# Attention, token mixing and gated convolution on one core: values' buffers written once, decoding apart from the sums, and a new order

## The chip, the core and the metric

One NeuronCore of a Trainium2 chip runs the whole program. Its engines work side by side, each on a queue of its own in program order: TensorE (PE, with PEld for its weight loads), VectorE (DVE), ScalarE (ACT), GpSimd (POOL) and SyncE (SP), which issues DMAs. The metric is the device time of one execution in microseconds; lower is better. The kernel before takes 675.87 us, the median of three runs (673.92 to 677.92).

## The reference

Four batches of eight heads with 576 tokens and 64 columns per head go through attention with a causal mask and a bias from cumulated sums; the heads' outputs are put side by side (512 columns), mixed over tokens, then over channels, then gated by a convolution over five tokens:

```python
scores = scale * q @ k.T + min(-(cum[:, None] - cum[None, :]), 0)   # causal
attn = softmax(scores);  x = concat_heads(attn @ v)
u = x + (relu(x.T @ w_tok1) @ w_tok2).T         # 576 -> 256 -> 576, over tokens
x = u + relu(u @ w_ch1) @ w_ch2                 # 512 -> 1536 -> 512
out = (sigmoid(conv5(x, conv_w)) * (x @ w_val)) @ w_out
```

The weights arrive as float64, two 32-bit words per number, and are decoded on the chip; q, k, v and s are float32. Products of float32 are made of three products of float16: each operand is split into a high part and a rest, scaled so that nothing underflows.

## The kernel before

**Tiles.** A batch b is worked as four pairs of heads (named b_0 to b_3), each over five tiles of at most 128 tokens; keys grow with the tile (causal). Batch 0's pairs are "wide": their product with v is a float32 one. A pair loads q, k and v, finds their largest values, scales and splits them (`qk16`, `v16`), transposes q and k by DMA (`turn_qk`, which gives `qkT` and `qk2`), writes a row of scales into `qk2` (`fill`), makes scores S on PE, masks and takes the maximum on DVE, exponentiates on ACT, splits p, transposes it (`p_turn`, tile pT; by DMA or on PE), and multiplies with v into the one PSUM bank `xbank` (`av`). `norm` reads the row sums out of xbank and inverts them on DVE; `x_value` multiplies. Then come token mixing (`tok1`, `tok2`), and for each batch two chunks of tokens (320 and 256, named b_0 and b_1) with the channel product: `u_split` (u from R, on DVE), `ch1` (matmuls `c<-u`), `ch2` (`c<-hT`), convolution and gate, `val` and `outp`.

**Weights.** A weight arrives in pieces `raw` of 128 rows with two words per number. `decode` (line 698) is given one piece: ACT scales the high word into `top` (a PSUM bank, or the weight's place in `arena` if the piece is longer than 512), ACT prepares the low word in place, DVE joins both into `arena`, PE sums the piece's columns with a matrix of ones (`ws_*<-arena,ones`, function `summed`, for the scale of the weight), and then the sign is put in: by DVE, or by ACT and a product on GpSimd. `scale` reads the sums' bank; `split` makes the high part and the rest.

**Values' buffers.** `load_v` of a wide pair takes a buffer of tag `v16`, has GpSimd write zeros into the rows behind the last token and ones into the 65th column (so that the product with v gives the row sums too), and then issues three DMAs on SP. A pair that is not wide loads v into `vst` and makes `v16` in `split_v`.

**What sets the order.** Every piece of work is a task, a generator that yields the engine of its next step. The text `ORDER` lists all steps by hand or search, an engine's letter and a task's number: V138 is the next step of task 138 on DVE. `Plan.run` replays it, so it is the program order of all five queues. Ahead of a step on PE, `keep_warm` compares the planned busy share of PE with `WARM_FILL` and puts filler matmuls in (`plan.idle`, line 524: `xbank<-ones`, 128x112, into columns 400 to 512 of xbank, which nobody reads). The dependency is kept for a tile, so a reader of xbank in program order behind a filler waits for the filler too. Where a task may choose its engine (`fillers`, `signed`, `one`, `two`), the letter in `ORDER` decides. The functions `cost_*` are the plan's own prices; they set how many fillers it inserts.

Everything that the engines are told goes through one call, so most rows of the profile carry line 256 (255 in the changed kernel); fillers carry 524 (525).

Of the kernel before, what the change touches and what calls it, by code (L numbers as in the profile page):

```python
# [8 lines left out]
F32 = mybir.dt.float32  # L9
# [9 lines left out]
SIGN = -(2 ** 31)  # L19
# [18 lines left out]
    fill=dict(V=(0.26, 130), A=(0.83, 200)),  # L38
# [14 lines left out]
WARM_FROM, WARM_FILL, GAP1 = 12e3, 0.65, 13.87  # L53
# [27 lines left out]
S6 S9 G138 S138 P7 A10 A10 V10 P10 A10 G10 S0 V0 P1 V1 V1 P1 V1 V1 S11 S17 A12 A12 A8 A8 V8 A2 A3 P8 V2 A3 A8 A2 V12  # L81
S137 A140 A140 A140 P12 V2 S20 V12 V3 P141 V141 V141 P141 V141 V141 V141 A142 V142 A143 V143 G8 V13 V13 V14 V14 S26
P18 A19 A19 V19 A21 A21 V21 P19 V19 P21 V21 V22 V22 P27 V25 S2 S139 S31 A28 A28 V28 G190 P28 S29 A30 A30 V30 A32 V28
A145 P30 V30 S191 A32 S144 S190 S144 P146 V146 P168 V168 P148 V148 A147 P154 V154 A169 P152 V152 A153 A155 P170 G4
S33 P160 V160 S189 S45 G24 G24 A149 V32 A34 S40 P174 V174 P177 P156 A156 P32 V32 A34 P156 A156 V177 A192 P150 A161
A150 A192 A192 G15 V34 V170 A171 P178 P175 V175 A176 P158 G5 G5 G5 G5 P34 V34 V35 V35 S43 P41 A46 P156 A156 P193
V193 P172 A172 V193 P151 P151 A42 P193 P172 A172 P157 V158 A159 V178 A179 V193 V193 V193 P157 G16 G16 P172 P162 A162
A46 V195 V194 V195 V194 P180 A180 S241 P162 A162 A42 V42 P162 A162 V197 P180 V46 A172 G15 P163 P163 V164 V164 V165
G23 A39 P42 P46 V46 A180 P180 A44 A44 V44 P173 P173 S47 A48 A48 P44 V42 S196 A180 P181 P181 G23 V44 V48 V166 V166
V182 V182 A183 G36 G37 P48 S196 P198 V198 A199 P212 V212 P200 V200 P206 V206 A184 A201 G37 S61 A48 S68 P167 A167  # L90
P204 V204 A205 V184 G36 G242 S242 P220 P226 V226 A213 P202 A207 P210 V210 P229 V229 G48 V49 A202 G39 V220 S54 P186
P186 A211 A186 V186 P230 P185 A185 P214 A214 S57 P227 V230 S59 V227 V49 A244 A244 A244 P187 P187 V187 V188 V188 P214
P55 A58 P245 V245 V245 P222 V222 S293 A214 P208 P245 V245 A208 V245 V245 V246 V188 V246 P69 P208 G247 V247 P214 A58
V58 S243 S248 S248 V249 A208 P208 A221 A208 A223 A228 P203 P203 P209 P209 P224 A214 P215 P215 V216 V216 V217 V218
V218 G50 A56 A231 G50 P232 G52 P58 V58 A224 P224 A56 V56 A232 A224 P232 A232 P224 A224 P232 A70 A70 V70 P219 P225
P225 P56 V56 P70 A232 P233 P233 G294 S294 S295 V70 S71 A60 A62 A62 V62 A60 V60 P62 A219 A38 G38 V234 V234 A235 P250
V250 A251 A51 P256 V256 A257 P258 V258 A259 P278 P281 V281 P264 V264 A265 P252 V252 A253 P60 V60 S73 S467 V62 S75
V278 P260 A260 P254 A236 V236 P260 A260 P272 V272 G53 P279 V279 P262 V262 A254 A296 G53 P274 V274 A296 P282 A273
P238 P238 V63 A296 P297 V297 V297 P297 V282 V297 S466 V297 V297 G299 A275 A72 A72 V72 P260 A260 V298 P255 P255 V299
P276 A263 P266 V298 P72 P261 P261 A280 V63 V65 S300 V67 A266 P266 V72 S77 G65 A74 A238 V238 S300 A74 V74 A266 P266  # L100
A283 P284 A266 P267 P267 V268 V268 A284 A76 A276 P276 A76 V76 A276 P284 A284 P237 V269 V270 V270 A237 A469 G66 P276
# [354 lines left out]
def gated_block_kernel(  # L456
# [241 lines left out]
    def decode(a, raw, tag, summed=None):  # L698
# [16 lines left out]
        if summed is not None:  # L715
            yield from summed()
        yield signed(n)
        x = ti if inner else raw[:, :, 1]
        if plan.engine is A:
            A.activation(low.bitcast(F32), x.bitcast(F32), AF.Sign)  # L720
            if inner:
# [1027 lines left out]
```

## Time and profile before

| | |
|---|---|
| median of three runs | 675.87 us (673.92 to 677.92) |
| profiled execution, time | 676.46 us |
| its span in the trace | 674.6 us (1.86 us outside) |
| PE busy | 616.4 us, 91%, 6040 matmuls |
| DVE busy | 509.1 us, 75%, 1400 |
| ACT busy | 383.9 us, 57%, 796 |
| GpSimd busy | 229.6 us, 34%, 336 |
| chain that ended last | PE 58%, DVE 15%, DMA 8%, ACT 4%, issue 3% |

Busy time is the union of an engine's instructions. PEclk is the share of TensorE's full clock (2.4 GHz) that was granted; 0.50 is 1.2 GHz. In a timeline row the number in brackets is the engine's idle time just before it, and what ended that. A buffer number is left out of a name, so `arena<-top,raw` stands for many pieces. The first channel product (`c<-u`) begins at 151.17 us; what lies before it is called the front.

### The profile page before, as it was taken

The numbers are of one execution on the slowest core, as the hardware profiler recorded it, in microseconds if no ns is written. First come the engines' busy times: TensorE is split into PE (matmuls) and PEld (weight loads), VectorE is DVE, ScalarE is ACT, GpSimd is POOL, SyncE is SP. The second block draws the span as 40 slices with busy tenths as digits, with TensorE's granted clock in tenths as the row PEclk, the third lists the DMA queues.
The fourth block names the chain that finished last, engine by engine and source line by source line (L and its number), as shares of the span: only waits on it lengthen the run. The fifth ranks groups of instructions, "written<-read, shape, count | busy, mean of one in ns | idle before, by whom it ended". The sixth has DMA issues, their size and how long they took to land.

```text
span 674.6 us, 15836 instructions
## 1 busy us (share of the span) xinstructions
PE 616.4 (91%) x6040; PEld 491.3 (73%) x6040; DVE 509.1 (75%) x1400; ACT 383.9 (57%) x796; POOL 229.6 (34%) x336
## 2 busy tenths in 40 slices
PE   2889889876999888999989999989999999999997
PEld 2678778764777777767767777767877887678864
DVE  5785799896898988758888978777779861456472
ACT  5694889785676747566575564546575611213324
POOL 2362248331554222441426224233373200037100
PEclk9996899998999999999999999999999999999999
DMA  7977278675856646773467365844654400000002
GB/s 211 218 203 221 60 185 228 177 160 116 218 88 102 132 97 119 126 144 90 97 111 141 64 116 117 153 86 100 125 106 85 94 21 1 17 1 1 2 32 95
DMA packets 190807, 75.18 MB, mean 111 GB/s; under 512 B 178213, under 2 KB 181381, under 8 KB 190730
## 3 DMA queue, kind: packets, MB, share of 16 engines
q1 hardware_dynamic: 190730, 74.16, 50.4%
q8 instruction: 47, 0.77, 0.5%
q14 instruction: 30, 0.25, 0.1%
HBM read 33.89 MB, written 4.83 MB: 57 GB/s over the span
## 4 chain that ended last, share of the span: by engine, by line
PE 58%; DVE 15%; DMA 8%; ACT 4%; issue 3%; SPq 2%; POOL 1%; DVEq 0%; POOLq 0%; ACTq 0%
PE c L256 32%; PE o L256 6%; PE xbank L256 5%; PE v L256 4%; PE t L256 4%; DMA pT<-p 4%; PE S L256 4%; DVE x L256 3%; DVE gate L256 3%; DMA qkT<-qk 2%; SPq L256 2%; DMA qk<-qkT 2%; DVE arena L256 2%; DVE qk L256 1%; ACT x L256 1%
## 5 line engine op out<-in xcount | busy, mean ns | idle before, releaser
L256 PEld LDWEIGHTS <-arena 128*128 128x128 f16 x3168 | 287.6, 98 | 74.8 <-issue 5.3
L256 PE MATMUL c<-hT,arena 128*128 128x256 f16 (+1 forms) x1152 | 159.2, 286 | 1.3 <-DVE st L256 1.3
L256 PE MATMUL c<-u,arena 128*128 128x256 f16 (+1 forms) x1152 | 158.4, 288 | 0.7 <-DVE u L256 0.5
L256 ACT ACTIVATE x<-x,st 128x320 f32<-128x320 f32 (+4 forms) x160 | 85.7, 556 | 74.8 <-DVE st L256 72.6
L256 POOL TENSOR_TENSOR p<-x,p 128x320 f16<-128x320 f32 (+4 forms) x78 | 60.7, 780 | 113.7 <-ACT p L256 80.5
L256 DVE CUSTOM_DVE_ANT_0 x<-S,mask,sc 128x448 f32<-128x448 f32 (+4 forms) x160 | 74.7, 485 | 26.2 <-PE S L256 15.6
L256 ACT ACTIVATE hT<-c 128x320 f16<-128x320 f32 (+1 forms) x96 | 36.7, 402 | 65.4 <-PE c L256 65.2
L256 PE MATMUL xbank<-v,pT 128*128 128x65 f16 (+1 forms) x880 | 64.9, 213 | 7.2 <-DMA pT<-p 7.0
L256 DVE SCALAR_TENSOR_TENSOR hT<-c,hT 128x320 f16<-128x320 f32 (+1 forms) x96 | 41.9, 449 | 33.7 <-ACT hT L256 33.7
L256 DVE SCALAR_TENSOR_TENSOR gate<-R,cwt,gate 128x320 f32<-128x320 f32 (+1 forms) x104 | 61.0, 601 | 1.5
L256 PE MATMUL S<-qk 67*128 67x288 f16 (+4 forms) x192 | 50.9, 286 | 5.3 <-DMA qk<-qkT 5.2
L256 PE MATMUL v<-x,arena 128*128 128x256 f16 (+1 forms) x384 | 53.6, 286 | 1.8 <-DVE st L256 1.8
L256 PE MATMUL S<-qkT 128*128 128x288 f16 (+4 forms) x192 | 50.8, 284 | 2.5 <-DVE hT L256 1.6
L256 PEld LDWEIGHTS <-pT 128*128 128x128 f16 x960 | 37.7, 98 | 12.8 <-DMA pT<-p 8.9
L256 PE MATMUL o<-arena,g 128*128 128x512 f16 x192 | 45.0, 379 | 0.0
L524 PE MATMUL xbank<-ones 128*128 128x112 bf16 x433 | 36.6, 231 | 4.5 <-DVE x L256 2.6
L256 POOL TENSOR_SCALAR p<-x 128x192 f16<-128x192 f32 (+4 forms) x40 | 17.2, 429 | 63.0 <-ACT x L256 36.4
L524 PEld LDWEIGHTS <-ones 128*128 128x128 bf16 x433 | 31.0, 110 | 6.8 <-issue 4.6
L256 ACT ACTIVATE p<-x 128x448 f16<-128x448 f32 (+4 forms) x65 | 31.7, 496 | 6.1 <-DMA pT<-p 4.5
L256 PEld LDWEIGHTS <-g 128*128 128x128 f16 x192 | 18.7, 99 | 18.2
L256 ACT ACTIVATE gate<-gate 128x1280 f32<-128x1280 f32 (+1 forms) x24 | 27.8, 1160 | 7.2 <-DVE gate L256 6.8
L256 PE MATMUL t<-xn,arena 128*128 128x128 f16 x480 | 30.4, 220 | 1.1 <-DVE hT L256 1.0
(204 smaller groups left out, 1091.2 us busy)
## 6 DMA issues: line engine op xcount, KB each, us to landing
raw<-in_moe_w_ch_dram SPq DMA_DIRECT2D x24, 512.0 KB
stg<-in_q_dram SPq DMA_DIRECT2D x16, 288.0 KB
stg<-in_k_dram SPq DMA_DIRECT2D x16, 288.0 KB
qk<-qkT SPq DMA_DIRECT2D x32, 144.0 KB
out_dram<-ot SPq DMA_DIRECT2D x16, 256.0 KB
vst<-in_v_dram SPq DMA_DIRECT2D x24, 128.0 KB
raw<-in_moe_w_val_dram SPq DMA_DIRECT2D x4, 512.0 KB
raw<-in_moe_w_out_dram SPq DMA_DIRECT2D x4, 512.0 KB
```

The lines of the kernel that those rows point to most:

```text
L256: return f(*a, **k)
L524: plan.idle = lambda: nc.tensor.matmul(xbank[:, 400:512], lhsT=ones, rhs=ones[:, 0:112], start=True, stop=True)
```

## The change

1. The two buffers of tag `v16` are allocated once (`v16s`), with a list of the free ones (`free_v`). A new task `t_v` writes the zeros and ones into both on GpSimd. `load_v` of a wide pair is left with its DMAs on SP; `largest` also waits for `t_v`.
2. `decode` writes the joined word into the raw piece in place, and only the step with the sign writes `arena`: on DVE from top and raw, or as a product on GpSimd of two words of raw, the second written by ACT. The sums on PE read the raw piece (its upper 16 bits, every fourth 16-bit word, before every second one of `arena`) and stand behind the sign's step in program order. The raw piece is given back after both.
3. `fill` may run on GpSimd; in the new order two fills go from ACT and three from DVE to GpSimd, three from ACT to DVE.
4. In the plan's prices a DMA transpose is longer (150 + 180 per block, before 100 per block), other DMAs move at 320 bytes per ns (360), a transposition on PE counts 0.4 as activity (0.6), and `WARM_FILL` is 0.75 (0.65).
5. `ORDER` is a new one, with 3457 steps (3461). The number of fillers goes from 433 to 514; ahead of the first channel product from 408 to 498. All other matmuls are the same in number and size.

```diff
-    fill=dict(V=(0.26, 130), A=(0.83, 200)),
+    fill=dict(V=(0.26, 130), A=(0.83, 200), G=(0.72, 285)),
...
-WARM_FROM, WARM_FILL, GAP1 = 12e3, 0.65, 13.87
+WARM_FROM, WARM_FILL, GAP1 = 12e3, 0.75, 13.87
...
-S6 S9 G138 S138 P7 A10 A10 V10 P10 A10 G10 S0 V0 P1 V1 V1 P1 V1 V1 S11 S17 A12 A12 A8 A8 V8 A2 A3 P8 V2 A3 A8 A2 V12
...
@@ decode
         yield V
-        V.scalar_tensor_tensor(ai, ti, 3, low, ALU.logical_shift_left, ALU.bitwise_or)
-        if summed is not None:
-            yield from summed()
+        V.scalar_tensor_tensor(low, ti, 3, low, ALU.logical_shift_left, ALU.bitwise_or)
         yield signed(n)
-        x = ti if inner else raw[:, :, 1]
         if plan.engine is A:
-            A.activation(low.bitcast(F32), x.bitcast(F32), AF.Sign)
+            high = raw[:, :, 1].bitcast(F32)
+            A.activation(high, ti.bitcast(F32), AF.Sign)
             if inner:
                 give("B")
             yield G
-            G.tensor_tensor(a, a, low.bitcast(F32), ALU.mult)
+            G.tensor_tensor(a, low.bitcast(F32), high, ALU.mult)
         else:
-            V.scalar_tensor_tensor(ai, x, SIGN, ai, ALU.bitwise_and, ALU.bitwise_or)
+            V.scalar_tensor_tensor(ai, ti, SIGN, low, ALU.bitwise_and, ALU.bitwise_or)
             if inner:
                 give("B")
+        if summed is not None:
+            yield from summed()
         give(tag)
...
-                x = a.bitcast(BF16).rearrange("p (n t) -> p n t", t=2)[:, :, 1]
+                x = raw.bitcast(BF16).rearrange("p n (w t) -> p n w t", t=2)[:, :, 0, 1]
...
+    v16s = [ap.tile([P, 4 * NK * DV], F16, tag=f"v16_{i}", name=f"v16_{i}") for i in range(BUFS["v16"])]
+    free_v = list(v16s)
+
+    def wide_v(t):
+        return t.bitcast(F32).rearrange("p (h n d) -> p h n d", h=2, n=NK)
...
+    def init_v():
+
+        for t in v16s:
+            yield G
+            G.memset(wide_v(t)[TAIL:, :, NK - 1, 0:D], 0.0)
+            G.memset(wide_v(t)[:, :, :, D:DV], 1.0)
...
-            yield G, "v16"
-            t = ap.tile([P, 4 * NK * DV], F16, tag="v16", name=f"v_{self.nm}", bufs=BUFS["v16"])
-            self.vst = t.bitcast(F32).rearrange("p (h n d) -> p h n d", h=2, n=NK)
-
-            G.memset(self.vst[TAIL:, :, NK - 1, 0:D], 0.0)
-            G.memset(self.vst[:, :, :, D:DV], 1.0)
-            yield SY
+            yield SY, "v16"
+            self.vt = free_v.pop(0)
+            self.vst = wide_v(self.vt)
```

How the order moves, at the places that the prediction speaks of. Names ending in a number are allocations; `sums_0` belongs to a pair's `norm`, `su` and `u_b_c` to a chunk's `u_split`, `S` and `x_4` to scores, `arena<-top,raw` and `raw<-top,raw` to decoding, `arena<-arena,wsgs` to splitting a weight.

DVE at the begin of batch 0's channel product, before:

```order
L256 SCALAR_TENSOR_TENSOR arena<-top,raw 128x512
L256 ISA x_4_2235,st_4_2089<-S_4_1_2325,mask,st_4_2089,sc_0_1706 128x288
L256 ISA st_4_2089 128x1
L256 SCALAR_TENSOR_TENSOR u_0_0_2358<-R_121,su_2283,u_0_0_2358 128x640 x2
L256 TENSOR_SCALAR sums_0_2444<-xbank,sc_0_1706 128x6
L256 SCALAR_TENSOR_TENSOR qk_1_1_2310<-stg_1_1650,sg_1_2223,qk_1_1_2310 128x9x64
```

DVE at the same place, after:

```order
L255 SCALAR_TENSOR_TENSOR raw<-top,raw 128x512
L255 TENSOR_SCALAR sums_0_2414<-xbank,sc_0_1666 128x6
L255 RECIPROCAL sg_1_2283<-gm_1_2282 128x3
L255 SCALAR_TENSOR_TENSOR arena<-top,raw 128x512
L255 SCALAR_TENSOR_TENSOR sc_1_2284<-sg_1_2283,gck 128x1
L255 SCALAR_TENSOR_TENSOR sc_1_2284<-gm_1_2282 128x1
L255 TENSOR_SCALAR sc_1_2284<-two_107,sg_1_2283 128x2
L255 SCALAR_TENSOR_TENSOR u_0_0_2422<-R_121,su_2323,u_0_0_2422 128x640 x2
L255 ISA x_4_2321,st_4_2105<-S_4_1_2358,mask,st_4_2105,sc_0_1666 128x288
L255 ISA st_4_2105 128x1
```

`sums_0`, the first `norm` of pair 1_0, stood behind both parts of `u_0_0` and now stands ahead of them.

PE in the channel product of chunk 0_0, between its third and fourth group, before:

```order
L256 MATMUL c_0_0_2_2413<-u_0_0_2358,arena 128x320
L524 LDWEIGHTS ones
L524 MATMUL xbank<-ones 128x112
L524 LDWEIGHTS ones
L524 MATMUL xbank<-ones 128x112
L256 LDWEIGHTS arena
L256 MATMUL c_0_0_3_2428<-u_0_0_2358,arena 128x320
```

and after:

```order
L255 MATMUL c_0_0_2_2518<-u_0_0_2422,arena 128x320
L255 LDWEIGHTS arena
L255 MATMUL c_0_0_2_2518<-u_0_0_2422,arena 128x320
L255 LDWEIGHTS arena
L255 MATMUL c_0_0_3_2534<-u_0_0_2422,arena 128x320
```

The two fillers between the groups are gone; in the order of before they are the last writers of xbank ahead of that `norm`.

DVE in the decoding of an early weight, before (piece after piece, with the sums of PE between the two kinds of rows):

```order
L256 TENSOR_REDUCE wpf<-ws_t_271 128x1
L256 TENSOR_SCALAR wpf<-wpf 128x1 x2
L256 RECIPROCAL wsg_t_359<-wpf 128x1
L256 TENSOR_SCALAR wsg_t_359<-wsg_t_359 128x1
L256 SCALAR_TENSOR_TENSOR ru_118<-wpf 128x1
L256 SCALAR_TENSOR_TENSOR arena<-top,raw 128x512 x2
L256 SCALAR_TENSOR_TENSOR arena<-top,arena 128x512 x2
L256 ISA x_0_449,st_0_450<-S_0_0_446,mask,sc_0_221 128x64
```

and after:

```order
L255 SCALAR_TENSOR_TENSOR qk_0_0_268<-stg_0_189,sg_0_240,qk_0_0_268 128x9x64 x2
L255 SCALAR_TENSOR_TENSOR raw<-arena,raw 128x576
L255 SCALAR_TENSOR_TENSOR arena<-arena,raw 128x576
L255 SCALAR_TENSOR_TENSOR raw<-arena,raw 128x576
L255 SCALAR_TENSOR_TENSOR arena<-arena,raw 128x576
L255 SCALAR_TENSOR_TENSOR raw<-top,raw 128x512
L255 SCALAR_TENSOR_TENSOR arena<-top,raw 128x512
L255 SCALAR_TENSOR_TENSOR raw<-top,raw 128x512
L255 SCALAR_TENSOR_TENSOR arena<-top,raw 128x512
L255 TENSOR_REDUCE wpf<-ws_t_284 128x1
```

The step with the sign (`arena<-top,raw`) now follows directly on the step that makes its operand (`raw<-top,raw`).

DVE at the channel product of batch 1, before:

```order
L256 TENSOR_SCALAR u_1_0_4611<-R_122,su_4524 128x640
L256 SCALAR_TENSOR_TENSOR u_1_0_4611<-R_122,su_4524,u_1_0_4611 128x640
L256 TENSOR_SCALAR sums_0_4625<-xbank,sc_0_3948 128x6
L256 SCALAR_TENSOR_TENSOR u_1_0_4611<-R_122,su_4524,u_1_0_4611 128x640
L256 RECIPROCAL sums_0_4625<-sums_0_4625 128x6
L256 TENSOR_TENSOR gm_1_4576<-xm,floor_95 128x3
L256 TENSOR_TENSOR p_16_4_4689<-x_4_4273,p_16_4_4689 128x9x64
L256 RECIPROCAL sg_1_4577<-gm_1_4576 128x3
L256 TENSOR_TENSOR p_16_3_4602<-x_3_4563,p_16_3_4602 128x7x64
```

and after:

```order
L255 TENSOR_SCALAR u_1_0_4694<-R_122,su_4601 128x640
L255 SCALAR_TENSOR_TENSOR u_1_0_4694<-R_122,su_4601,u_1_0_4694 128x640 x2
L255 TENSOR_TENSOR gm_1_4630<-xm,floor_95 128x3
L255 RECIPROCAL sg_1_4631<-gm_1_4630 128x3
L255 TENSOR_SCALAR sums_0_4763<-xbank,sc_0_4009 128x6
L255 TENSOR_TENSOR p_16_4_4771<-x_4_4360,p_16_4_4771 128x9x64
L255 SCALAR_TENSOR_TENSOR sc_1_4632<-sg_1_4631,gck 128x1
L255 SCALAR_TENSOR_TENSOR sc_1_4632<-gm_1_4630 128x1
L255 TENSOR_SCALAR sc_1_4632<-two_107,sg_1_4631 128x2
L255 TENSOR_SCALAR qk_2_1_4777<-stg_1_4422,sg_1_4631 128x9x64
L255 SCALAR_TENSOR_TENSOR qk_2_1_4777<-stg_1_4422,sg_1_4631,qk_2_1_4777 128x9x64 x2
```

The first `norm` of pair 2_0 (`sums_0`) stood between the two parts of the rest of `u_1_0` and now stands behind them and behind `gm` and `sg` of pair 2_1.

PE in the channel product of chunk 1_0, between its second and third group, before:

```order
L256 LDWEIGHTS arena
L256 MATMUL c_1_0_1_4642<-u_1_0_4611,arena 128x320
L256 LDWEIGHTS arena
L256 MATMUL c_1_0_2_4656<-u_1_0_4611,arena 128x320
L256 LDWEIGHTS arena
```

and after:

```order
L255 MATMUL c_1_0_1_4713<-u_1_0_4694,arena 128x320
L255 LDWEIGHTS arena
L255 MATMUL c_1_0_1_4713<-u_1_0_4694,arena 128x320
L525 LDWEIGHTS ones
L525 MATMUL xbank<-ones 128x112
L255 LDWEIGHTS arena
L255 MATMUL c_1_0_2_4728<-u_1_0_4694,arena 128x320
L255 LDWEIGHTS arena
```

A filler, a writer of xbank, now stands between the groups.

## Rows read from the trace of the kernel before

**Rows 1.** The page's busy line: engine, busy us, share of the span, instructions.

```profile
PE 616.4 (91%) x6040; PEld 491.3 (73%) x6040; DVE 509.1 (75%) x1400; ACT 383.9 (57%) x796; POOL 229.6 (34%) x336
```

**Rows 2.** Stages: start:end, length, busy us (count) of each engine, PEclk, DMA, GB/s.

```profile
0.00:15.00 15.00, 1.98 (x20) 1.75 (x21) 6.97 (x26) 7.17 (x14) 3.50 (x12) 1.00 0.78 221
15.00:152.00 137.00, 118.67 (x1248) 104.69 (x1246) 115.43 (x338) 106.44 (x241) 58.88 (x79) 0.93 0.72 181
152.00:170.00 18.00, 12.74 (x81) 8.57 (x81) 12.77 (x24) 11.16 (x24) 4.19 (x6) 0.81 0.50 111
170.00:282.00 112.00, 104.14 (x1142) 84.33 (x1140) 99.56 (x279) 72.20 (x150) 43.69 (x68) 1.00 0.65 128
282.00:674.60 392.60, 378.91 (x3558) 291.97 (x3556) 274.39 (x736) 186.97 (x370) 119.36 (x172) 1.00 0.39 79
```

**Rows 3.** Fillers alone (line 524 on PE) ahead of the first channel product.

```profile
0.00:152.00 152.00, 33.68 (x408) 0.93 0.72 185
```

**Rows 4.** Waits: who waits for whom, us in total, times, longest us.

```profile
PE xbank L256 <- DMA pT<-p: 7.0, 8, 1.6
...
DVE arena L256 <- PE ws_c L256: 5.5, 5, 2.5
...
DVE arena L256 <- PE ws_wv L256: 1.8, 1, 1.8
```

**Rows 5.** Timeline of DVE, 43 to 54 us: start, us, instruction, idle before.

```profile
43.29 2.59 DVE L256 SCALAR_TENSOR_TENSOR qk<-stg,sg,qk 128x576 f16<-128x576 f32 x2
...
53.65 0.69 DVE L256 SCALAR_TENSOR_TENSOR arena<-top,arena 128x512 int32<-128x512 int32 x1 [2.50 <-PE ws_c L256]
```

**Rows 6.** Timeline of DVE around its longest wait on PE.

```profile
150.26 1.68 DVE L256 SCALAR_TENSOR_TENSOR u<-R,su,u 128x640 f16<-128x640 f32 x2
157.09 0.23 DVE L256 TENSOR_SCALAR sums<-xbank,sc 128x6 f32<-128x6 f32 x1 [5.16 <-PE xbank L524]
157.23 0.81 DVE L256 SCALAR_TENSOR_TENSOR qk<-stg,sg,qk 128x576 f16<-128x576 f32 x1
```

**Rows 7.** Timeline of PE at the same place.

```profile
153.53 3.42 PE L256 MATMUL c<-u,arena 128*128 128x320 f16 x24
156.79 0.26 PE L524 MATMUL xbank<-ones 128*128 128x112 bf16 x2
156.89 1.79 PE L256 MATMUL c<-u,arena 128*128 128x320 f16 x12
163.94 0.58 PE L256 MATMUL ws_wv<-arena,ones 128*128 128x128 bf16 x4 [5.26 <-DVE arena L256]
```

**Rows 8.** Stages around the two stretches of half clock, columns as rows 2.

```profile
46.40:49.60 3.20, 1.33 (x18) 1.19 (x17) 2.44 (x7) 2.55 (x5) 0.00 (x0) 0.99 0.86 164
49.60:63.20 13.60, 13.60 (x73) 12.11 (x72) 7.51 (x25) 4.66 (x15) 2.66 (x5) 0.50 0.61 178
...
162.20:169.00 6.80, 5.06 (x24) 3.14 (x24) 6.76 (x13) 6.01 (x14) 2.59 (x4) 0.50 0.23 45
169.00:175.00 6.00, 6.00 (x51) 4.41 (x50) 4.13 (x9) 1.87 (x6) 5.55 (x9) 1.00 0.54 124
```

**Rows 9.** Groups by form: busy us, mean ns of one, idle before.

```profile
L256 ACT ACTIVATE qk<-one,sc 3x1152 f16<-3x1152 f16 x13 | 16.2, 1247 | 1.6 <-DVE sc L256 1.3
...
L256 POOL TENSOR_SCALAR qk<-stg,sg 128x576 f16<-128x576 f32 x5 | 3.9, 776 | 22.1 <-DVE sg L256 22.1
...
L256 POOL MEMSET v<- 64x128 f32 x4 | 0.8, 201 | 23.2 <-PE xbank L256 12.8 <-issue 10.3
```

**Rows 10.** Timeline of GpSimd beside rows 5.

```profile
43.72 1.54 POOL L256 TENSOR_TENSOR arena<-arena 128x512 f16<-128x512 f32 x1
```

**Rows 11.** Timeline of PE with fillers and sums, 25 to 28 us.

```profile
25.04 1.78 PE L524 MATMUL xbank<-ones 128*128 128x112 bf16 x33
27.76 0.39 PE L256 MATMUL ws_c<-arena,ones 128*128 128x128 bf16 x4 [0.94 <-DVE arena L256]
27.99 0.31 PE L524 MATMUL xbank<-ones 128*128 128x112 bf16 x3
```

## What the change does to the time: the prediction

> **What bounds the kernel now.** I read the busy line first, then the span by stages, then the waits, then the two timelines around the largest wait. TensorE is busy 91% of the span and no other engine over 75% [rows 1]. That is an average over unlike stages, and the stage rows are what counts [rows 2]. From 170 to 674.6 us PE is busy 104.14 of 112 and 378.91 of 392.6 us at full granted clock: only 21.6 us are idle there, so nothing but fewer matmuls or closed gaps can shorten that part, and the useful matmuls are the same before and after. The time is to be had before 170. In the first 152 us PE is busy 1.98 + 118.67, but 33.68 of it are the 408 filler matmuls [rows 3]; useful work is 87 us. DVE is busy 6.97 + 115.43 and ACT 7.17 + 106.44. No engine is the bound: the front is a chain through decoding, scores, softmax and transposes, in which DVE is mostly the next link. From 152 to 170 PE is busy 12.74 of 18.
>
> Two things are visible in these first 170 us. One is waiting. DVE waits 5.5 us for the weights' sums on PE, five times, the longest 2.50 [rows 4, 5]. And at 151.94 DVE stops for 5.16 us [rows 6]: the next step in its queue is the first normalisation of attention pair 1_0, which reads xbank; the last writers of xbank ahead of it are two fillers that stand on PE after the third group of the channel product (156.79, [rows 7]). PE pays it back: it has two more groups queued, runs dry, and then waits 5.26 us for a sum whose decoding stood behind the normalisation on DVE. The other thing is TensorE's clock. After 46.4 to 49.6, where PE was busy 1.33 of 3.20 us, the granted clock is 0.50 (1.2 GHz) for 13.6 us with PE busy all the time; after the 5.26 us idle it is 0.50 again from 162.2 to 169 with PE busy 5.06, and 1.00 behind it [rows 8].
>
> **The change, part by part**, against the profiled execution (676.46: span 674.6 and 1.86 around it; the median of the runs is 675.87, so its results are lowered by 0.6 at the end).
>
> *Zeros and ones once.* Each wide pair had two GpSimd memsets, the larger 201 ns [rows 9]; eight become four. GpSimd is busy 62 of the first 152 us [rows 2], so at most 0.8 us of its work goes where it idles: 0. Loads of wide pairs no longer queue behind GpSimd. No wait of PE or DVE on that load stands among the large ones: 0.
>
> *The fill by GpSimd.* Two fills leave ACT (1.25 us each [rows 9]), three leave DVE. A fill on GpSimd is not in the trace; nearest above is its scale row over 576 elements of 128 partitions, 0.78, so twice the length gives about 1.6; nearest below is ACT's 1.25. Neither end is on a path: 0. With every moved step priced at the mean of its like in the trace, DVE gets 5 us more, POOL 8 more, ACT 15 less, against 509, 230 and 384 [rows 1]. The 5 us lie mostly past 170, where DVE is busy 99.56 of 112 and 274.39 of 392.6 [rows 2]: cover is there, thin at first.
>
> *GpSimd and DVE together.* At 43.29 two steps of DVE on q and k took 2.59 us while GpSimd worked on a subtraction (43.72, 1.54); the same step alone took 0.81 [rows 5, 6, 10]. So 8 us more GpSimd work can cost DVE between 0 and about 0.6 of it, 4.8 us; DVE idles a quarter of the span, so I take 0 and keep 3 for the range. The Trainium skill, "SBUF — State Buffer", section "SBUF: two separate sides", has a reason: the two engines share a pair of ports, and one instruction holds it whole. By that rule all 8 us could fall on DVE, and the sum would be 668 where DVE's idle time hides them and up to 676 where it doesn't, which is the second rival below; the stretched pair agrees with its direction.
>
> *Decoding apart from the sums.* DVE's second step no longer waits for PE's sum of the first. This takes away the 5.5 us of waits on DVE (and 1.8 on the values' weights), in 0 to 152. What is late next: the wait was in part shadowed, because scores and softmax come to DVE in turn. In exchange, 15 pairs of dependent DVE steps now stand back to back; in the timeline independent steps overlap by some 0.09 (157.09 and 0.23 long, the next at 157.23, [rows 6]), and a dependent one can't, so 15 x 0.1 = 1.5 us more. Net on DVE 4 us; I take half as reaching the end of the front: **-2** (bounds -5.5 and 0). The first of the ACT steps and GpSimd's product read raw words with a stride; they stay with their group's time: 0.
>
> *The strided sums.* The sums now read every fourth 16-bit word. Before, it was every second: four of them take 0.39 us, and the next row begins 0.23 behind [rows 11], 58 ns each. No row has the new stride. Below nothing is excluded, since the same number of columns is read; above, doubling costs 152 x 58 ns = 8.8 us of PE, two thirds in the front. I take 0: the rate with every second word is that of the dense fillers (54 ns for 112 columns, 62 for 128). The Trainium skill, "SBUF — State Buffer", section on Door 1, says that a stride is free while two reads fall in one 16-byte line, which this one just keeps; by it the sum is also 0.
>
> *Fillers.* 433 become 514; ahead of the first channel product 408 become 498. One costs 54 ns at full clock [rows 11], 83 in the mean of the front [rows 3]: 90 are 4.9 to 7.5 us of PE. PE idles 18 us from 15 to 152 [rows 2], and most of them fall there. On the path: **+1** (0 to 7.5). They are there for the clock: if 46.4 to 49.6 is filled, the 13.6 us at half clock are 6.8 at full. But the fillers follow the plan's idea of where PE is idle, not the real one: the plan of before had this gap too. I take **-2** (0 to -6.8).
>
> *The order at 152.* The normalisation of 1_0 moves ahead of the split of u and needs only its own attention product, since no filler stands between; in the channel product of batch 0 the fillers between the groups are gone. The 5.16 us on DVE go; late next is the same sum, one to two DVE steps (0.7 each) behind PE: **-4.5** (-3 to -5.3). Without the idle stretch the clock has no cause to fall: of 5.06 us at half clock half come back, **-2** (0 to -2.5).
>
> *The order after 170.* The distance from each score to the product that needs its transposed probabilities, counted in PE's work, is on average the same. PE waits for these transposes 7.0 us in all [rows 4]. But a filler now stands after the second group of batch 1's channel product, and the first normalisation of pair 2_0, right behind the split of u on DVE, waits for it: the same trap in a new place. Between lie about two groups of 12 matmuls at full clock, 3.3 us by the 24 from 153.53 to 156.89 [rows 7]. Queued behind on DVE: the lower part of a probability tile, then q and k of pair 2_1, so its transposes come late. PE has matmuls of the channel product queued for longer than that: 0 to 3.3, I take **+1.5**. Elsewhere 0, within ±4.
>
> Sum: -2 + 1 - 2 - 4.5 - 2 + 1.5 = -8. 676.5 - 8 = 668.5, less 0.6 is **668**. The case's own range: with the wait at 152 gone and the clock full behind it in every end, the front between -6 and 0, the rest ±4, 660 to 673.
>
> **Rivals.** *Only the wait goes.* The front is a chain; fillers eat what the sums gave, and the slow clock at 49.6 stays: -4.5 + 1.5 and half of the clock's 2 is -4, so **672**. For it: the waits for sums are 5.5 us spread over five places and DVE idles 137 - 115.43 = 21.6 us from 15 to 152. *Shift eaten.* The pipeline of batches 1 to 3 is held by DVE (89% busy from 170 to 282), with 5 us more to do; work that came early waits for it, and the end stays at **676**. Against it: PE has 21.6 us idle only. *Slower: the fillers.* PE is made nearly the bound in the front: 118.67 + 7.5 = 126 of the 137 us from 15 to 152. If fillers stand in front of the matmul that the chain waits for, and some meet the half clock (108 ns each, 9.7 us in all), then +9 on the path, no gain at the sums or the clock, -4.5 at 152 and +1.5 at 2_0: 676.5 + 6 - 0.6, about **682**. It decides once more than half of the added fillers delay a real matmul. For it: PE was busy all of 49.6 to 63.2 already. *It doesn't do what it says:* the normalisation could still wait for a filler; the order of the program shows none between, so this has no share of its own.
>
> **Chances.** The forecast 0.54, only the wait 0.20, eaten 0.13, slower 0.13. A measurement can tell 0.5% from no change, 672.5 and 679.3 here. The forecast gives 0.51 faster and 0.03 same; only the wait 0.11 and 0.09; eaten 0.01, 0.10 and 0.02 slower; fillers 0.02 same and 0.11 slower. Faster 0.63, same 0.24, slower 0.13. The range 659 to 680 leaves out some 0.04 below and 0.10 above.
>
> **What would show it.** Right: no wait of DVE on a filler near the end of the front; PE without a 5 us gap there, granted clock 1.00 behind it; DVE without waits on the sums; the first channel product begun some 3 us earlier; the sums at 58 ns each; a wait of DVE on a filler of about 3 us near 280 with little on PE. Wrong: the sums at 100 ns or more; the first channel product later than 151; PE gaps past 170 above 22 us; half clock for longer than 13.6 us around 50.

## The result, and the profile after

The changed kernel takes **653.64 us** (652.76 to 653.86, four runs) where the kernel before, run beside it, takes 676.64: a ratio of **0.9663** (95% interval 0.963 to 0.9695), 22.8 us. The prediction said 668 with a range of 659 to 680: the direction was right, the size a third of what came, and the time lies below the range. Times of the experiments below are given as such ratios to the kernel before on the same chip, and a difference in microseconds by 1% = 6.77 us; a time is the median of the run's own executions. These medians can differ by a few tenths of a per cent from one chip to the next, so two runs are compared by their ratios.

The profiled execution has a span of 651.9 us (674.6 before). The busy line of its page, to set beside [rows 1]:

```profile
PE 615.6 (94%) x6121; PEld 496.4 (76%) x6121; DVE 503.7 (77%) x1407; ACT 371.0 (57%) x790; POOL 239.6 (37%) x344
```

PE's busy time is the same, though there are 81 more matmuls; what went is idle time, 58.2 us before and 36.3 after. The next two views show where. They are stages of before and of after, cut at the same points of the program: begin of the scores of pair 0_1, of the channel products of chunks 0_0, 0_1 and 1_0, and the end (columns as in rows 2).

```profile
0.00:58.10 58.10, 39.12 (x389) 35.38 (x390) 39.83 (x118) 35.45 (x72) 20.76 (x38) 0.90 0.79 206
58.10:151.20 93.10, 81.27 (x876) 70.98 (x875) 81.83 (x245) 77.36 (x181) 41.63 (x54) 0.95 0.69 172
151.20:186.20 35.00, 29.21 (x253) 20.91 (x251) 26.67 (x59) 21.74 (x49) 13.52 (x19) 0.90 0.68 165
186.20:291.50 105.30, 96.81 (x1053) 78.14 (x1051) 93.68 (x269) 67.79 (x137) 35.96 (x57) 1.00 0.63 111
291.50:674.60 383.10, 370.03 (x3478) 285.89 (x3476) 267.12 (x711) 181.60 (x360) 117.77 (x170) 1.00 0.38 77
```

```profile
0.00:50.00 50.00, 36.83 (x416) 33.67 (x417) 40.38 (x119) 34.15 (x72) 23.63 (x40) 1.00 0.88 229
50.00:140.70 90.70, 84.12 (x939) 76.67 (x937) 79.17 (x241) 73.24 (x171) 44.71 (x57) 0.98 0.72 183
140.70:170.70 30.00, 27.53 (x249) 20.53 (x247) 29.22 (x65) 22.73 (x52) 10.94 (x15) 1.00 0.75 172
170.70:269.40 98.70, 95.74 (x1053) 78.63 (x1052) 88.03 (x259) 69.08 (x140) 41.11 (x61) 1.00 0.67 126
269.40:651.90 382.50, 371.36 (x3473) 286.86 (x3471) 266.92 (x726) 171.85 (x359) 119.21 (x173) 1.00 0.37 77
```

The five stages change by -8.1, -2.4, -5.0, -6.6 and -0.6 us. By the first channel product 10.5 us are gained (the prediction: 3), through chunk 0_0 another 5.0 (6.5 with the clock), in the next 105 us 6.6 and in the last 380 almost nothing (together +1.5 predicted). PE's idle time in the last two stages goes from 21.6 to 14.1 us. The granted clock of the first stage goes from 0.90 to 1.00 as far as it is recorded: neither profile has a record of it before some 20 us, and ahead of that a filler takes about 100 ns in both kernels (17 in 1.77 us from 15.16 before, 10 in 0.94 from 14.66 after), the pace of half clock. DVE's busy time, which the prediction had 5 us longer, is 5.4 shorter.

The largest single loss of before is gone as predicted. DVE in the changed kernel at the place of rows 6:

```profile
138.03 0.22 DVE L255 TENSOR_SCALAR sums<-xbank,sc 128x6 f32<-128x6 f32 x1
...
139.15 1.68 DVE L255 SCALAR_TENSOR_TENSOR u<-R,su,u 128x640 f16<-128x640 f32 x2
```

The normalisation of 1_0 (`sums`) stands ahead of the split of u and waits for nothing.

### The profile page after: what moved, and what is told of

Read it like the earlier page. It is cut to its first block, busy times and chain, and to the rows that moved or that the text cites. A ratio compares the mean times of both kernels' runs of the same rounds, so it can differ in the third digit from the quotient of the medians.

```text
span 651.9 us, 16028 instructions
## 1 busy us (share of the span) xinstructions
PE 615.6 (94%) x6121; PEld 496.4 (76%) x6121; DVE 503.7 (77%) x1407; ACT 371.0 (57%) x790; POOL 239.6 (37%) x344
## 4 chain that ended last, share of the span: by engine, by line
PE 69%; DVE 13%; DMA 7%; ACT 3%; issue 2%; SPq 2%; POOL 2%; DVEq 0%; ACTq 0%; POOLq 0%
PE c L255 34%; PE o L255 7%; PE xbank L255 6%; PE t L255 5%; PE S L255 5%; PE v L255 5%; DMA pT<-p 3%; DMA qkT<-qk 2%; DVE qk L255 2%; DVE x L255 2%; SPq L255 2%; DMA qk<-qkT 2%; PE xbank L525 1%; DVE gate L255 1%; PE xT L255 1%
## 5 line engine op out<-in xcount | busy, mean ns | idle before, releaser
L255 ACT ACTIVATE x<-x,st 128x192 f32<-128x192 f32 (+4 forms) x160 | 86.2, 556 | 68.1 <-DVE st L255 58.7
L255 POOL TENSOR_TENSOR p<-x,p 128x64 f16<-128x64 f32 (+4 forms) x79 | 65.1, 827 | 76.9 <-ACT p L255 60.7
L255 PE MATMUL xbank<-v,pT 128*128 128x65 f16 (+1 forms) x880 | 62.0, 208 | 7.0 <-DMA pT<-p 4.2
L255 DVE SCALAR_TENSOR_TENSOR gate<-R,cwt,gate 128x320 f32<-128x320 f32 (+1 forms) x104 | 55.5, 551 | 1.1
L255 PE MATMUL S<-qk 67*128 67x192 f16 (+4 forms) x192 | 49.3, 278 | 2.0 <-DMA qk<-qkT 1.8
L255 PE MATMUL S<-qkT 128*128 128x192 f16 (+4 forms) x192 | 49.2, 277 | 1.0 <-DVE st L255 0.8
L255 POOL TENSOR_SCALAR p<-x 128x192 f16<-128x192 f32 (+4 forms) x48 | 23.4, 488 | 68.4 <-ACT x L255 36.4
L525 PEld LDWEIGHTS <-ones 128*128 128x128 bf16 x514 | 34.5, 107 | 8.2 <-issue 6.6
L255 ACT ACTIVATE p<-x 128x576 f16<-128x576 f32 (+4 forms) x52 | 25.6, 496 | 11.0 <-DMA pT<-p 9.8
L255 PE MATMUL xbank<-vsw,pT 128*128 128x65 f16 x240 | 30.4, 195 | 0.0
```

The source lines that it names most:

```text
L255: return f(*a, **k)
L525: plan.idle = lambda: nc.tensor.matmul(xbank[:, 400:512], lhsT=ones, rhs=ones[:, 0:112], start=True, stop=True)
```

## The experiments

Three theories stood at first: F (the added fillers keep the clock full), D (decoding apart from the sums) and O (the new order).

**Fillers.** e1 gives the kernel before the new plan's prices and fill share; e2 gives the changed kernel the old ones.

```diff
-WARM_FROM, WARM_FILL, GAP1 = 12e3, 0.65, 13.87
+WARM_FROM, WARM_FILL, GAP1 = 12e3, 0.75, 13.87
...
```

> The kernel before, its order and all else kept, with the plan's prices and the fill share of the changed kernel: 594 fillers instead of 433. Theory F (the fillers keep the clock full, and that is the front's gain of 10 us): no stretch of half clock near 50 us, the first channel product some 8 to 10 us earlier than 151, time 666 to 669 us. Theory D (decoding apart from the sums is the gain) and theory O (the new order is): the fillers change little, 674 to 679 us.

> The changed kernel with the plan's prices and the fill share of before: 381 fillers instead of 514. Theory F: a stretch of half clock comes back between 35 and 60 us, the first channel product 6 to 10 us later than 140.7, time 660 to 664 us. Theories D and O: 652 to 656 us.

e1: 1.000 (0.9954 to 1.0047). e2: 0.9602 (0.9562 to 0.9641), if anything faster than the changed kernel. In e1's trace the half clock near 50 us is gone, and the first channel product still begins at 148.9 instead of 151.2; in e2's the clock stays full from 35 to 60 us. Theory F falls.

**Decoding.** e3 gives the kernel before the new decoding, e4 the changed kernel the old one, each with its own order but for the place of the sums (tokens of the order, here for one piece in e3; e4 the other way). In these runs, and in all below, a list `FILLS` holds the number of fillers ahead of each step on PE, so that the fillers stay as they were where the edit isn't about them:

```diff
-A10 A10 V10 P10 A10 G10
+A10 A10 V10 A10 G10 P10
...
     def keep_warm(self, until):
...
+        for _ in range(int(FILLS[self.pes])):
+            self.idle()
+        self.pes += 1
```

> The kernel before with the new decoding alone: in place, sums on the raw piece, each piece's sums moved in the order to right behind the sign's last step; all else in its order, and the fillers ahead of each step on PE as before. Theory D: DVE's 7.3 us of waits on sums go and the front ends 4 to 8 us earlier, time 668 to 672 us. Theories F and O: 674 to 678 us; the half clock near 50 stays.

> The changed kernel with the old decoding alone: the joined word in the arena, its sums ahead of the sign's step, which waits for them; all else in its order, and the fillers ahead of each step on PE as in the changed kernel. Theory D: DVE waits for sums by 5 us or more, time 658 to 662 us. Theories F and O: 653 to 656 us.

e3: 1.0068 (1.0025 to 1.0112), slower; e4: 1.0012 (0.9982 to 1.0043), all 23 us lost. Neither expectation of D fits: alone the decoding costs 4.6 us (1.7 to 7.6), and yet the new order can't do without it. The waits of DVE in e4:

```profile
DVE arena L276 <- PE ws_wo L276: 8.9, 4, 4.7
...
DVE arena L276 <- PE ws_c L276: 8.7, 14, 2.1
...
DVE arena L276 <- PE ws_wv L276: 7.2, 4, 3.3
```

The sign's step writes the arena, where PE reads the sums, and the new order has the two DVE steps back to back, so DVE waits each time until PE's queue has come to the sum: 24.8 us in these three rows. To see whether that wait or the sums' earlier place on PE is the cause, r2 keeps the early place but leaves the sums on the raw piece:

```diff
+        if summed is not None:
+            yield from summed()
         yield signed(n)
...
-        if summed is not None:
-            yield from summed()
         give(tag)
```

> The changed kernel with the sums' step ahead of the sign's step in the order, as in e4_after_old_decode, but still on the raw piece, which the sign's step on DVE only reads. Theory W (what costs 26 us in e4 is that the sign's step writes where the sums read, so DVE waits for PE): no such wait here, 652 to 657 us. Theory Q (what costs is the sums' earlier place in PE's queue, where PE waits for DVE): 668 to 680 us.

r2: 0.9768 (0.968 to 0.9856), 7 us above the changed kernel and 16.5 below e4. DVE's sign step waits for no sum there; instead PE's sums wait for the joining step, which they do for 1.1 us in the changed kernel:

```profile
PE ws_c L276 <- DVE raw L276: 6.7, 6, 2.4
```

So both theories hold a part, the write into what PE reads the larger; how large each is stays rough, as r2's interval is 12 us wide.

**The wait at 152.** e5 moves one step of the kernel before, the token V497:

```diff
-A347 A349 V349 A348 V348 P350 P350 P352 P352 P354 P354 P356 P356 G506 S506 V497
+A347 A349 V497 V349 A348 V348 P350 P350 P352 P352 P354 P354 P356 P356 G506 S506
```

> The kernel before with one step moved: the first normalisation of pair 1_0 ahead of the split of u of chunk 0_0; fillers step by step as before. By the prediction the 5.16 us wait of DVE, the idle stretch of PE and the half clock behind it go: 4.5 + 2 us, 669 to 672 us. The rival (the next pair's chain is late anyway and takes them back): 674 to 678 us.

e5: 0.9902 (0.9865 to 0.9939), **-6.6 us**, as the prediction had it. DVE and PE at the place of rows 6 and 7:

```profile
148.88 0.22 DVE L276 TENSOR_SCALAR sums<-xbank,sc 128x6 f32<-128x6 f32 x1
149.02 1.67 DVE L276 SCALAR_TENSOR_TENSOR u<-R,su,u 128x640 f16<-128x640 f32 x2
```

```profile
155.64 1.79 PE L276 MATMUL c<-u,arena 128*128 128x320 f16 x12
157.31 0.39 PE L276 MATMUL ws_wv<-arena,ones 128*128 128x128 bf16 x4
```

The fourth group of PE ends and the sums follow without a gap; at half clock there is nothing behind it. The stage from the first channel product to that of chunk 0_1, 35.00 us before:

```profile
150.20:178.70 28.50, 26.90 (x255) 19.87 (x252) 26.46 (x58) 21.59 (x48) 13.00 (x19) 1.00 0.87 204
```

PE's idle time there falls by 4.2 us (5.8 to 1.6) and its busy time by 2.3 (29.21 to 26.90), where the prediction had 4.5 for the wait and 2 for the clock.

**The new trap.** e6 takes one filler out of the changed kernel, the one ahead of the third group of chunk 1_0: in its `FILLS` the number at the step P708 is 0, in the changed kernel it is 1; all others stay.

> The changed kernel without the one filler ahead of the third group of chunk 1_0's channel product. By the prediction this filler costs 0 to 3.3 us: DVE's wait of 3.9 us on it goes and the time is 651 to 653 us. The rival (what it delays has slack): 653 to 655 us, with the wait gone all the same.

e6: 0.9583 (0.9556 to 0.961), 648.5 us: **5.4 us** for one matmul of 54 ns, more than the 0 to 3.3 expected. In the changed kernel DVE, then PE:

```profile
267.10 1.66 DVE L255 SCALAR_TENSOR_TENSOR u<-R,su,u 128x640 f16<-128x640 f32 x2
...
272.93 0.22 DVE L255 TENSOR_SCALAR sums<-xbank,sc 128x6 f32<-128x6 f32 x1 [3.89 <-PE xbank L525]
...
277.91 0.18 DVE L255 RECIPROCAL sums<-sums 128x6 f32<-128x6 f32 x1
```

```profile
269.42 3.42 PE L255 MATMUL c<-u,arena 128*128 128x320 f16 x24
272.68 0.21 PE L525 MATMUL xbank<-ones 128*128 128x112 bf16 x1
...
279.57 0.28 PE L255 MATMUL xbank<-v,pT 128*128 128x65 f16 x4 [2.55 <-ACT x L255]
```

DVE waits 3.89 us for the filler at 272.68. Behind it on DVE stand q and k of pair 2_1 and then the rest of the norm (277.91), so the values of pair 2_0 come late, PE waits 2.55 us at 279.57 for ACT to read xbank, and the granted clock is 0.50 for 3.4 us behind that. In e6 the same step:

```profile
270.49 0.20 DVE L277 TENSOR_SCALAR sums<-xbank,sc 128x6 f32<-128x6 f32 x1
```

**Front and rest.** h1 and h2 mix the two orders at the first matmul of chunk 0_1; r4 cuts at that of chunk 1_0. In all three the program is the changed one; of h1 the order is

```diff
-the changed kernel's ORDER
+ORDER of before up to the first step of ch1 of chunk 0_1
+the changed kernel's ORDER, without the steps that are done
```

and of h2 and r4 the other way round.

> The changed program in a mixed order: up to the first matmul of chunk 0_1's channel product the steps and fillers of before (with the sums behind the sign), from there what is left in the changed kernel's order. Theory S (two gains that add: 15.5 us up to that matmul, 7.4 us after it by the order of the rest): the front as in e3_before_new_decode, that matmul near 191, then the rest of the changed kernel, 481 us: 673 to 676 us. Theory P (the rest is faster only because the front hands over more work done): 679 to 683 us.

> The same mix the other way: the changed kernel's steps and fillers up to the first matmul of chunk 0_1's channel product, from there what is left in the order of before. Theory S: that matmul at 170.7, then the 490 us of before: 659 to 663 us. Theory P: the rest as fast as in the changed kernel, 652 to 656 us.

> The changed program in the changed order up to the first matmul of chunk 1_0's channel product (269.4 us), from there what is left in the order of before. From that matmul to the last chunk's values product the changed kernel takes 363.0 us and the one before 363.7. If the rest's order brings nothing: 652 to 656 us. If what h2_after_front_before_rest lost against the changed kernel (9 us) lies in how the orders fit at the seam and not in what stands between the two seams: 659 to 664 us.

h2: 0.9786 (0.9758 to 0.9814), as theory S has it: with the new front, the old rest costs 8.3 us. r4: 0.9708 (0.9648 to 0.9769), 3.0 us, between its two expectations, with an interval that reaches into both, so that r4 alone shows no loss against the changed kernel. That most of what the rest gains lies between the two cuts is what the stages show (6.6 of 7.2 us); r4 agrees with it. h1: 1.0052 (1.0023 to 1.008), only 1.1 us better than e3 with the same front: on the old front the new rest brings little. In its trace the seam itself costs (DVE waits 4.2 us there for a scale and PE 4.8 for transposes), so h1 doesn't tell S from P.

**Zeros once, and the two joined.** r3 has of the change `v16s`, `init_v` and what `load_v` and `split_v` do with them, r1 joins e2 and e6.

```diff
-            yield G, "v16"
+            yield SY, "v16"
+            self.vt = free_v.pop(0)
```

> The kernel before with the values' buffers allocated and written once, and nothing else changed; the fillers step by step as before. By the prediction 0: 674 to 679 us. The rival (the loads of v freed from GpSimd's queue start the front earlier): 670 to 673 us.

> The changed kernel with the fillers that the prices of before give (as e2_after_fewer_fillers), and without the three of them ahead of the third group of chunk 1_0's channel product (as e6_after_no_filler_in_chunk): 378 fillers. If the two gains add (2.1 and 5.1 us), 645 to 648 us; if the fewer fillers only had an effect through that one place, 648 to 650 us.

r3: 1.000 (0.9968 to 1.0032), nothing, as predicted. r1: 0.9559 (0.9507 to 0.9612), not to be told from e6. By its median, 649.6 us, the two do not add; by its ratio, 7.0 us below the changed kernel, they would (2.1 and 5.1). The interval covers both, so this stays open.

**What binds the front.** That left the front's 10 us without a cause. x4 and x5 issue eight steps of DVE twice:

```diff
         V.scalar_tensor_tensor(low, ti, 3, low, ALU.logical_shift_left, ALU.bitwise_or)
+        if again:
+            V.scalar_tensor_tensor(low, ti, 3, low, ALU.logical_shift_left, ALU.bitwise_or)
```

> The changed kernel with DVE's joining step of the eight pieces of c11 and c12 (43 to 79 us) issued twice, which changes no value: 8 x 0.68 = 5.4 us more on DVE in the front, nothing else. Theory B (the front is bound by DVE, so that what DVE loses or gains there passes to the end in full): 658 to 661 us. Theory C (the front is a chain through all engines and DVE has slack; half or less passes, as the prediction took it): 653 to 656.5 us.

> The same eight steps issued twice in the kernel before: 5.4 us more on DVE between 46 and 93 us. Theory B: 681 to 685 us. Theory C: 676 to 680.5 us.

x4: 0.9721 (0.9674 to 0.9768), +3.9 us. x5: 1.0049 (1.0016 to 1.0081), +3.3. By these values a share of 0.6 to 0.7 of the 5.4 us passes to the end in both kernels, a little more than the half that the prediction took and between B and C; the intervals (1.1 to 5.5 us for x5) exclude neither.

x3 puts the five fills of the front back:

```diff
-G146 ... G198 ... G250 ... G302 ... G475
+A146 ... V198 ... V250 ... A302 ... V475
```

> The changed kernel with the five fills of pairs 0_0 to 1_0 off GpSimd and on the engines where they were before (two on ACT, three on DVE), at the same places of the order. By the prediction 0: 652 to 655.5 us. Theory B: three times 0.72 us more on DVE in the front and 1.25 us on ACT ahead of the first scores, 655.5 to 658 us.

x3: 0.9797 (0.9755 to 0.9839), **+9.1 us**, twice the most that theory B gave. y2 is the reverse, the kernel before with its five fills on GpSimd:

> The kernel before with the five fills of pairs 0_0 to 1_0 on GpSimd, at the same places of the order. Theory T (the fills stand in the front's chain, and the PE gap of 1.7 us near 47 that the clock falls after is theirs, as x3_after_front_fills_back made one of 2.4 us in the changed kernel): the 13.6 us at half clock go, 666 to 672 us. Theory N (this counts only in the new order): 673 to 679 us.

y2: 0.9854 (0.981 to 0.9898), **-9.9 us**. Its first channel product begins at 141.6; 151.2 before, 140.7 in the changed kernel. Taken back and put in, the five fills are worth what the front gained: their place is its cause. One way in which a step of 0.51 us does it is seen in the kernel before. DVE, then PE:

```profile
46.52 0.51 DVE L256 TENSOR_SCALAR qk<-qk,sc 3x1152 f16<-3x1152 f16 x1
47.05 0.69 DVE L256 SCALAR_TENSOR_TENSOR arena<-top,raw 128x512 int32<-128x512 int32 x1
...
48.08 0.56 DVE L256 TENSOR_TENSOR x<-xbank,sums 128x384 f32<-128x384 f32 x1
```

```profile
46.54 0.41 PE L256 MATMUL ws_c<-arena,ones 128*128 128x128 bf16 x4
48.69 0.31 PE L524 MATMUL xbank<-ones 128*128 128x112 bf16 x3 [1.74 <-DVE x L256]
```

The fill (`qk<-qk,sc`, 46.52) and a join stand on DVE ahead of `x_value`, which reads xbank at 48.08. PE's next item is a filler, which writes xbank, and so PE waits 1.74 us for DVE. It is the gap of rows 8: PE busy 1.33 of 3.20 us, and then 13.6 us at half clock. The changed kernel's DVE at this place has no fill and no join before it:

```profile
41.61 0.75 DVE L255 SCALAR_TENSOR_TENSOR arena<-arena,wsg_c 128x512 f16<-128x512 f32 x1 [0.82 <-POOL arena L255]
42.27 0.16 DVE L255 TENSOR_SCALAR sums<-xbank 128x6 f32<-128x6 f32 x1
...
42.69 0.56 DVE L255 TENSOR_TENSOR x<-xbank,sums 128x384 f32<-128x384 f32 x1
```

And the two windows around it, in the changed kernel, in y2 and in x3:

```profile
42.30:45.50 3.20, 2.26 (x28) 2.19 (x27) 2.78 (x8) 3.20 (x7) 3.11 (x5) 1.00 1.27 151
45.50:59.10 13.60, 13.60 (x145) 12.40 (x145) 12.39 (x48) 9.54 (x26) 8.21 (x9) 1.00 0.92 269
```

```profile
46.40:49.60 3.20, 2.35 (x30) 2.23 (x28) 2.21 (x6) 3.20 (x8) 3.02 (x4) 1.00 0.67 128
49.60:63.20 13.60, 12.77 (x134) 11.11 (x132) 12.01 (x41) 9.07 (x26) 9.52 (x12) 1.00 0.87 251
```

```profile
42.50:45.80 3.30, 0.95 (x16) 0.82 (x14) 3.17 (x7) 2.24 (x5) 1.88 (x4) 0.99 1.24 151
45.80:59.40 13.60, 13.60 (x74) 12.32 (x73) 7.67 (x21) 3.96 (x10) 7.47 (x8) 0.50 0.51 146
```

Behind the windows with PE busy 2.26 or 2.35 of 3.20 us the granted clock reads 1.00, and in the next 13.6 us PE gets through 145 or 134 matmuls and DVE works 12 us. Behind the one with 0.95 busy (x3), as behind that with 1.33 before, it reads 0.50: 74 or 73 matmuls, all of PE's time taken, and DVE works 7.7 or 7.5 us. The gap alone doesn't make the fall, though. e1 has the fill in place and nearly the same gap, and its clock stays at 1.00 there (to 63.40):

```profile
48.93 0.31 PE L526 MATMUL xbank<-ones 128*128 128x112 bf16 x3 [1.69 <-DVE x L256]
```

What the clock and what the gaps are worth can be read from the first scores of pair 0_0 to those of 0_2, where PE has the same matmuls before and in y2, and again in the changed kernel and in x3. In this order before, e1, y2, the changed kernel and x3:

```profile
28.80:85.20 56.40, 49.77 (x443) 44.31 (x441) 42.60 (x120) 38.11 (x91) 24.17 (x30) 0.82 0.64 166
```

```profile
30.00:82.30 52.30, 43.58 (x478) 39.57 (x476) 41.84 (x120) 38.95 (x94) 23.98 (x33) 0.97 0.73 181
```

```profile
29.30:77.10 47.80, 43.27 (x446) 37.95 (x443) 40.78 (x119) 37.78 (x90) 27.72 (x33) 0.93 0.76 196
```

```profile
28.70:74.00 45.30, 42.06 (x430) 38.60 (x427) 38.67 (x119) 35.14 (x83) 23.65 (x27) 0.96 0.78 197
```

```profile
27.80:82.10 54.30, 47.78 (x428) 43.36 (x425) 40.69 (x121) 36.43 (x85) 21.26 (x25) 0.84 0.65 164
```

Nearly all of the 9.9 and 9.1 us lies here. Of y2's 8.6 us, 6.5 are PE's busy time, the same matmuls at a higher clock, and 2.1 its idle time; of x3's 9.0, 5.7 and 3.3. But the clock without the move is worth less than half: in e1 it is 0.97 with the fills in place, PE's busy time is as short as in y2 though 36 fillers more are in it, and its idle time grows from 6.6 to 8.7 us, so only 4.1 us are gained here, and 2.3 by the first channel product. PE then waits for others instead of being slow.

x2 takes all fillers out of the changed kernel, y1 out of the one before: every number of their `FILLS` is 0.

> The changed kernel without any filler. If the fillers are what keeps the clock full in the front: stretches of half clock through most of the first 140 us, and as useful matmuls are some 80 us of it at full clock, 665 to 690 us. If a front bound by DVE doesn't need them: 648 to 656 us, with half clock shown in the front all the same.

> The kernel before without any filler. Theory G (fillers cost more than the clock gives back: they hold PE where the clock is half, and make the normalisation of 1_0 wait): the 5.16 us wait goes as in e5_before_norm_early (669.7), and some us in the front with it, 662 to 670 us. Theory K (the old order needs them for the clock): 676 to 690 us.

x2: 0.9579 (0.9525 to 0.9632), 647.0 us; y1: 0.9827 (0.978 to 0.9873), -11.7 us. Both kernels are faster without a single filler, and with half clock in more of the front than before. x2 and e6 agree, so in the changed kernel the other 513 fillers together bring and cost nothing that can be measured; of y1's gain, 5.7 us lie in the stage through chunk 0_0 (29.3 us for 35.0), where the wait at 152 is gone. By its trace y1, with the fills where they were, begins the scores of 0_2 at 76.3, as early as y2 (77.1; 85.2 before): up to there the fills are dear only together with the fillers, which wait for xbank behind them. x2 and e6 beat both kernels.

## Why the prediction came out as it did

**Right.** The wait at 152 and the clock behind it: -6.5 predicted, -6.6 in e5, and the split is right too (4.2 and 2.3 by its trace). The text has PE with two more groups behind the fillers; the row shows one (12 matmuls, [rows 7]), which changes no term. Zeros once: 0 (r3). The fill's own price on GpSimd, 1.25 to 1.6:

```profile
L255 POOL TENSOR_SCALAR qk<-one,sc 3x1152 f16<-3x1152 f16 x5 | 7.0, 1409 | 1.6 <-PE xbank L525 1.3
```

The new wait of `norm` on a filler was foreseen at its place, 272.9 us; its price, +1.5 in the sum, was 5.4 (e6). The reason given, that PE has matmuls queued for longer, failed: the late step was the norm's own second half, and PE ran dry at 277.0 to 279.6.

**Wrong, the step that failed most: "Neither end is on a path: 0" for the fill.** It was worth 9 to 10 us (x3, y2), which is the front. The prediction had the gap in front of the slow clock (rows 8) and gave it to the lack of fillers ("They are there for the clock"). It did not ask what ended that gap. The timeline names DVE, and the two steps ahead on DVE's queue are the fill and a join. The size of a step on a queue was taken for its price; what counted was who waited behind it, and the clock at which PE went on. The bound of 6.8 us that the prediction gave to the clock is near the 6.5 us by which PE's busy time fell in y2; but the sum took 2 of it and expected it from fillers, and e1 shows that the clock which fillers keep is worth 2.3 us by the first channel product and nothing at the end.

**Fillers: +1, and -2 for the clock.** Both terms were near nothing in the sum, but the picture behind them was wrong. e1's added fillers kept the clock and gained nothing at the end, and without any both kernels are faster (x2, y1). Their cost is the dependency: they write xbank, so a reader or a writer of it waits (1.74 us near 47, 5.16 at 152, 3.89 at 269).

**Decoding: -2, by the waits that the old order had.** e3 measured +4.6 and e4 23.6 the other way. The prediction counted waits that go, and they did go: in the changed kernel DVE waits for no sum. But alone that gains nothing (e3); what the change does is to allow an order in which the two steps follow each other. The sums' price, which e3 and the changed kernel pay, was taken as 0 by a row with another stride. Four sums now take 0.62 us, and eight are 0.90 apart from what follows:

```profile
25.50 1.08 PE L255 MATMUL ws_c<-raw,ones 128*128 128x128 bf16 x8 [0.46 <-DVE raw L255]
26.40 1.31 PE L525 MATMUL xbank<-ones 128*128 128x112 bf16 x23
```

That is 112 ns each, against 58 before [rows 11], which the prediction had among its signs of being wrong and as its upper bound: for the 128 sums of 128 columns it is 128 x 54 ns = 6.9 us of PE at full clock. The Trainium skill, "SBUF — State Buffer", section on Door 1, has this stride as free; the measurement at full clock says double. How much of it reaches the end was not tried apart, and neither was the term for GpSimd and DVE together (0).

**After 170: +1.5, "elsewhere 0, within ±4".** By the traces -7.2, with the trap of 5.4 in it. PE's waits for transposes are shorter. From the first channel product of chunk 0_1 to the end, before and after:

```profile
PE xbank L256 <- DMA pT<-p: 5.6, 7, 1.6
PE S L256 <- DMA qk<-qkT: 3.8, 4, 1.4
```

```profile
PE xbank L255 <- DMA pT<-p: 4.2, 4, 1.8
PE xbank L255 <- ACT x L255: 2.6, 1, 2.6
PE S L255 <- DMA qk<-qkT: 1.2, 1, 1.2
```

The middle row of after is the trap. The prediction compared the distance from a score to its product on average; that the waits come from the shortest distances is the likely fault, and no run shows it. Between chunks 0_1 and 1_0 the gain is made of waits of up to two microseconds in several places; which step of the order removes each was not tried, and h1 leaves open how far they need the new front. This part is not settled.

**The rivals** named the same two parts as the forecast and no larger gain; a case in which a cheap step holds up the chain was not among them, which is why the range ended 5 us above the time.

In sum: the front's fills -9.9 (y2) and the wait at 152 -6.6 (e5) are 16.5 of 22.8 us, each measured in the kernel before. The remaining 6.3 are a difference and not a measurement: h2 gives 8.3 for the order of the rest, net of the trap of 5.4 (e6), and e3 a loss of 4.6 for the decoding, and nothing shows that the parts add. The decoding has no gain of its own; without it the new order loses everything (e4).

## What to carry to other kernels

Before an instruction that moves to another engine is priced at nothing, ask of each of them what stands behind it on the queue and which engine waits for that, and read for each fall of the clock which wait came before it. Filler matmuls are better off in a tile that nothing else reads or writes (not tried here; without fillers both kernels are faster): a dependency through a shared bank cost 5.4 us for a matmul of 54 ns. Two steps of one engine are only worth putting back to back if no other engine has to read between them what the second overwrites; an edit that removes such a bond can be worth nothing until the order uses it.

## What the runs showed of the hardware

- A matmul of 128 bf16 columns whose moving operand is read at a stride of 8 bytes takes 112 ns, at 4 bytes 58 ns, both at full clock. At half clock there is little between them: 115 ns (x3, four from 49.57, the next row at 50.03) and 107 (before, four from 52.98, the next row at 53.41).
- x2 is at half clock until 42.5 us as far as its matmuls show, and its front is 5 us shorter than the changed kernel's (135.6 for 140.7). The granted clock of a stretch reads 1.00 until the first change is recorded (at 42.5 us there); that it is half is seen in the matmuls, 448 columns from the first row to the second in 0.35 us, where 320 take 0.14 at full clock (3.36 us for 24, [rows 7]):

```profile
29.53 0.56 PE L277 MATMUL S<-qkT 128*128 128x448 f16 x1
29.88 0.58 PE L277 MATMUL S<-qk 67*128 67x448 f16 x1
30.25 0.37 PE L277 MATMUL S<-qkT 128*128 128x192 f16 x1
```
